# An attention and feed-forward kernel on Trainium2: another order of loads, output additions and remainders at the turns of batches and half batches

## The chip, the cores and the metric

The kernel runs on one core of one Trainium2 chip, as one program of 14,752 profiled instructions. The metric is the device time of one execution in microseconds (us); less is better.

## What is computed

For 8 batches, 8 heads, 576 tokens and a head width of 64, 32 memories per head are formed with softmax weights of `phi`; each token attends to these memories, and the result (4608 x 512) goes through a feed-forward layer (512 to 2048 to 512). All arrays are float32.

```python
a = exp(phi - max(phi, axis=2)); a = a / (sum(a, axis=2) + 1e-9)
k_m, v_m = einsum('bhsm,bhsd->bhmd', a, k), einsum('bhsm,bhsd->bhmd', a, v)
attn = softmax(q @ k_m.T / 8)                 # over the 32 memories
x = (attn @ v_m).transpose(0, 2, 1, 3).reshape(4608, 512)
h = x @ w_in
g = h * clip(h + 3, 0, 6) / 6
out = g @ w_out
```

## The kernel before, in words

**Order.** Every engine executes its instructions in the order in which the program issues them, and that order is written by hand: strings of words such as `fo.C.3` or `fetch.N.0.0` are played as calls. In the tables `FOURTH`, `STEADY` and `EVERY` the numbers are slots 0 to 31 of a batch; C is the batch in work, N the next one, M the one after. `FOURTH` belongs to batch 3, `STEADY` to batches 4 to 7, `EVERY` to all of these; words of batches past the last are dropped. SP (SyncE) issues the DMAs in the same order, so a DMA that waits holds back those behind it. PE is TensorE, DVE is VectorE, ACT is ScalarE, POOL is GpSimd.

**What a slot does.** From batch 3 on (287 us into the span) the loop over `s` (line 1039) makes one slot for each of the 16 blocks of 128 hidden columns in each half batch: slots 0 to 15 for the first half (256 tokens), 16 to 31 for the second (320 tokens, of which 64 are put by). Two slots (k = 0 and 1) make a unit. A slot's order is:

- `gemm1` (L716, six products on TensorE) into one of two PSUM banks; `relu` (L722, ScalarE) and `gate` (L735 and, for the 64 tokens, L739, VectorE);
- in an odd slot `sum_first` (L745, VectorE) and `sum_second` (L749 and L750, GpSimd): sums of the gated blocks for a fast 2 x 2 block multiplication with seven products A11, M5, M2, A22, M6, M7, M1;
- in an even slot `finish_unit(..., 1)` of the unit before, ahead of the slot's words; in an odd slot `finish_unit(..., 0)` of its own unit, behind the slot's words. `finish_unit` splits blocks into a rounded high part (L756, ScalarE) and its remainder (L761, VectorE): three blocks for part 0, which need `sum_first` alone, four for part 1, which need `sum_second` too;
- the words of the slot;
- `half_step(s - 3)`: the products (L688) of the unit three slots back, nine matmuls for part 0 in an odd slot, twelve for part 1 in an even slot. Each of the seven products is a `triple`: high x high, high x low, low x high, so the remainder is needed at the third matmul. Part 1 also fetches the streamed weights (L684) of the unit two ahead; M6, M7 and M1 read such streams. At the turns (slots 0 to 3 and 16 to 19) nothing is fetched, since the next half begins with the units that are still there.

**Leaving.** After a half batch's last unit the sums leave PSUM: `leave_first` in slot 1 or 17, `leave_second` (L795 on ScalarE, L798 and L799 on VectorE) and `leave_third` (L803 and L804 on GpSimd, then the store L806 on SP) in slot 2 or 18, so ahead of slot 3's or 19's `sum_second` on GpSimd. The next half's products take the same four PSUM banks.

**Batches 4 and 6.** In their slots 0 to 2 and after slot 2 the products of the tokens put by are made (`rest_stage`). There the words of slots 0, 1 and 2 are played after its units 3, 4 and 5, and `leave_third` after its unit 2.

**The words that the change moves.** `fetch.N.c.h` (L217) loads half h of weight chunk c (512 KB) from DRAM into one of two buffers: chunks 0 and 2 share one, 1 and 3 the other; `fo` (L428, TensorE) folds the next batch's values into a chunk, `vh` (L439, ScalarE) and `vl` (L448, VectorE, one operand in PSUM) split the result; `bh` (L412, ScalarE) and `bl` (L417, GpSimd) split the second half's probabilities; `xa` (L309, and L306 twice for `xa.N.2`, VectorE) and `xe` (L313, ScalarE) are phi less its maxima and its exponential; `pn` (L225) and `kv` (L238) load phi and k and v; `mt` (L277, VectorE) and `mo` (L283, SP) turn and write out phi's maxima, `sp` (L288, SP) reads them back; `cs` (L391, GpSimd) and `ds`, `dr`, `dm` (L403, GpSimd) belong to the attention's softmax.

## Time and profile before

| | |
|---|---|
| runs | 1340.69, 703.06 and 705.54 us; median 705.54 |
| profiled execution | 705.24 us, of which the span of instructions is 703.2 |
| TensorE busy | 680.7 us, 97% of the span |
| VectorE, ScalarE, GpSimd busy | 532.1, 388.1, 333.0 us |
| granted clock of TensorE | 0.998 on average |
| DMA | 162.86 MB, 232 GB/s |

The profile is of one execution. Times count from the first instruction. In the view of stretches a row is: stretch, its length, busy time of the engine with the number of its instructions, granted clock of TensorE (1.00 is full speed), busy share of the DMA engines, GB/s. In the timeline a row is: start, length, engine, line of the kernel, operation, output<-inputs, shapes, number of instructions merged; in brackets the idle time before it and what ended that. A VectorE or GpSimd instruction that is held up after its start shows a greater length and no idle time. "SPq" is SyncE's queue at the issue of a DMA. The view of waits has: who waited for whom, us in total, times, longest. Slot 0 of batch 5 begins at 452.25, of batch 7 at 615.71; slot 4 of batch 5 at 462.67, of batch 7 at 624.42; slot 5 of batch 4 at 389.66.

### The profile page before, as it was taken

To read this page: it belongs to the slowest core of one execution; us is meant where nothing else is said; L and a number is where in the kernel's file an instruction comes from. 1 tells how busy PE (TensorE), PEld (TensorE's weight loads), DVE (VectorE), ACT (ScalarE), POOL (GpSimd) and SP (SyncE) were. 2 spreads that over 40 slices of the span, in tenths; PEclk is the share of its full clock that TensorE was granted. 3 is DMA by queue.
4 is the path that set the end of the run, shared out by engine and by line. 5 is a ranking of instruction groups with operands and counts; after the bars stand their busy time and mean duration, and the time that the engine had idled before them with its cause. 6 is when DMAs were issued, how large, how long until landed. Compare 5 with 4: busy or idle time off the path is not lost.

```text
span 703.2 us, 14752 instructions
## 1 busy us (share of the span) xinstructions
PE 680.7 (97%) x5622; PEld 577.2 (82%) x5622; DVE 532.1 (76%) x962; ACT 388.1 (55%) x786; POOL 333.0 (47%) x333
## 2 busy tenths in 40 slices
PE   8999999999999999999999999899999999999997
PEld 3456777878877787789889998799988999889997
DVE  4899987776466455566998869977898778987765
ACT  4677785554344455554655655555465555655543
POOL 2645330396564574632545435453457334554433
PEclk9999999999999999999999999999999999999999
DMA  9988573655671784899673877749675593736351
GB/s 353 421 328 314 181 270 125 225 178 178 270 260 47 277 291 132 302 375 343 221 260 118 265 273 271 275 166 332 216 262 191 155 323 114 270 118 219 121 180 47
DMA packets 66270, 162.86 MB, mean 232 GB/s; under 512 B 6808, under 2 KB 13976, under 8 KB 63640
## 3 DMA queue, kind: packets, MB, share of 16 engines
q1 hardware_dynamic: 66120, 161.86, 65.2%
q8 instruction: 44, 0.72, 0.4%
q14 instruction: 26, 0.21, 0.1%
q10 hardware_dynamic: 80, 0.07, 0.0%
HBM read 135.68 MB, written 26.22 MB: 230 GB/s over the span
## 4 chain that ended last, share of the span: by engine, by line
PE 47%; DVE 27%; DMA 9%; ACT 7%; issue 4%; POOL 3%; SPq 2%; ACTq 0%; POOLq 0%; DVEq 0%
PE acc L688 17%; PE acc L545 11%; PE ph L491 7%; PE ph L716 7%; DVE rounded L761 7%; DVE gated L735 3%; DVE gated L745 3%; DVE both L448 2%; DMA stream<-kept 2%; DMA w<-w_kept 2%; ACT rounded L756 2%; PE pk L323 2%; DMA kvt<-in_kv 2%; PE pv L428 2%; DMA kept<-stage 1%
## 5 line engine op out<-in xcount | busy, mean ns | idle before, releaser
L688 PE MATMUL acc<-w,rounded 128*128 128x256 f32 x1248 | 177.7, 282 | 4.4 <-DVE rounded L761 3.8
L688 PEld LDWEIGHTS acc<-w,rounded 128*128 128x128 f32 x1248 | 157.7, 188 | 26.7 <-issue 10.8
L749 POOL TENSOR_TENSOR gated<-gated 128x256 f32<-128x256 f32 x80 | 76.8, 961 | 189.0 <-DVE gated L735 158.2
L761 DVE TENSOR_TENSOR rounded<-gated,rounded 128x384 fp32r<-128x384 f32 (+1 forms) x160 | 133.2, 833 | 38.0 <-ACT rounded L756 32.5
L716 PE MATMUL ph<-probs,both 128*128 128x256 f32 (+1 forms) x960 | 150.4, 292 | 0.0
L756 ACT CAST rounded<-gated 128x384 fp32r<-128x384 f32 (+1 forms) x160 | 90.6, 567 | 95.3 <-DVE gated L745 89.2
L716 PEld LDWEIGHTS ph<-probs,both 128*128 128x128 f32 x960 | 131.6, 188 | 0.2
L722 ACT ACTIVATE gf<-ph,three 128x256 f32<-128x256 f32 (+1 forms) x160 | 79.9, 499 | 42.3 <-PE ph L716 40.7
L545 PE MATMUL acc<-w,ghi 128*128 128x512 f32 x384 | 101.0, 398 | 0.1
L688 PE MATMUL acc<-stream,rounded 128*128 128x256 f32 x720 | 97.3, 279 | 1.5 <-DMA stream<-kept 1.3
L688 PEld LDWEIGHTS acc<-stream,rounded 128*128 128x128 f32 x720 | 88.6, 188 | 3.6 <-DMA stream<-kept 2.5
L545 PEld LDWEIGHTS acc<-w,ghi 128*128 128x128 f32 x384 | 68.9, 188 | 23.9 <-issue 5.7
L735 DVE SCALAR_TENSOR_TENSOR gated<-gf,ph 128x256 f32<-128x256 f32 x160 | 65.5, 410 | 27.0 <-ACT gf L722 26.9
L491 PEld LDWEIGHTS ph<-probs,both 128*128 128x128 f32 x528 | 75.0, 188 | 11.2 <-DVE gf L507 5.2
L491 PE MATMUL ph<-probs,both 128*128 128x256 f32 (+1 forms) x528 | 78.5, 297 | 2.7 <-DVE gf L507 2.6
L507 DVE SCALAR_TENSOR_TENSOR gf<-gf,ph 128x576 f32<-128x576 f32 x44 | 33.0, 750 | 40.8 <-ACT gf L501 40.6
L501 ACT ACTIVATE gf<-ph,three 128x576 f32<-128x576 f32 (+2 forms) x52 | 36.5, 703 | 43.0 <-PE ph L491 38.1
L545 PE MATMUL acc<-w,glo 128*128 128x512 f32 x192 | 54.0, 390 | 0.0
L448 DVE TENSOR_TENSOR both<-pv,both 128x512 fp32r<-128x512 f32 x62 | 42.3, 682 | 14.9 <-ACT both L439 14.7
L525 DVE TENSOR_TENSOR glo<-gf,ghi 128x512 fp32r<-128x512 f32 x44 | 39.1, 892 | 12.8 <-PE acc L545 7.0
L439 ACT CAST both<-pv 128x512 fp32r<-128x512 f32 x62 | 36.1, 584 | 20.7 <-DVE both L448 13.6
L194 POOL TENSOR_TENSOR w<-tmp,raw 128x512 uint32<-128x512 uint32 x14 | 21.8, 1580 | 45.2 <-DVE tmp L184 24.5
(106 smaller groups left out, 886.9 us busy)
## 6 DMA issues: line engine op xcount, KB each, us to landing
stream<-kept SPq DMA_DIRECT2D x186, 256.0 KB, 4.4
kvt<-in_kv SPq DMA_DIRECT2D x32, 516.0 KB, 7.0
w<-w_kept SPq DMA_DIRECT2D x32, 512.0 KB, 6.0
raw<-in_w SPq DMA_DIRECT2D x16, 512.0 KB, 8.6
raw<-in_w SPq DMA_DIRECT2D x8, 1024.0 KB, 7.9
out_t<-o SPq DMA_DIRECT2D x16, 512.0 KB, 3.3
w<-w_kept SPq DMA_DIRECT2D x8, 1024.0 KB, 7.8
kept<-stage SPq DMA_DIRECT2D x24, 256.0 KB, 4.4
```

The source lines that it names most:

```text
L448: nc.vector.tensor_tensor(both[:, 1], src, both[:, 0].bitcast(F32), ALU.subtract)
L491: nc.tensor.matmul(dst, w[:, g, fs], x[:, g * n : (g + 1) * n], start=(i == 0), stop=(i == len(seq) - 1),)
L501: nc.scalar.activation(self.gf, self.h, AF.Relu, bias=three)
L525: nc.vector.tensor_tensor(self.glo[:, :n], self.gated(), self.ghi[:, :n].bitcast(F32), ALU.subtract)
L545: nc.tensor.matmul(accs[self.b, self.rest, k].rearrange("p (x c) -> p x c", c=VC), left[:, t * P : (t + 1) * P], w, start=k in self.first ...
L688: nc.tensor.matmul(dst, left[l], right[r], start=begin and n == 0, stop=end and n == 2, skip_group_check=True)
L716: nc.tensor.matmul(h, w[:, g, fs], x[:, g * self.n : (g + 1) * self.n], start=(i == 0), stop=(i == len(seq) - 1))
L722: nc.scalar.activation(self.gf, self.h[k], AF.Relu, bias=three)
L735: nc.vector.scalar_tensor_tensor(dst, by_tile(self.gf), 6.0, by_tile(self.h[k]), ALU.min, ALU.mult)
L749: nc.gpsimd.tensor_tensor(g[:, 2:4], g[:, 0::8], g[:, 1:8:6], ALU.subtract)
L756: nc.scalar.copy(self.parts[0][:, at], self.g[:, 1:8][:, at])
L761: nc.vector.tensor_tensor(low[:, at], self.g[:, 1:8][:, at], high[:, at].bitcast(F32), ALU.subtract)
```

## The change

Eight edits, all of order; the number and the sizes of the instructions stay.

- The loads of the next batch's first two weight chunks go from slots 5, 7, 9 and 11 to slots 0, 1, 1 and 2 (batches 4 to 7), in batch 3 to 7, 9, 11 and 16. The last half of the fourth chunk goes from slot 29 to 27.
- `vl.C.3.0` goes from slot 0 to 1, `vh.C.3.1` from 3 to 4, `vl.C.3.1` from 4 to 5, `bh.C.1` from 4 to 6, `bl.C.1` from 5 to 7.
- `xa.N.0` goes from 6 to 5, `xe.N.0` from 7 to 6, `xa.N.1` and `xa.N.2` from 8 to 7, `xe.N.1` from 9 to 8.
- `pn.M` goes from 20 to 17, `mt.M` and `mo.M` from 27 to 29, `kv.M.2` from 27 to 28.
- Part 1's products are in the order M6, M7, A22, M1 instead of A22, M6, M7, M1.
- In `leave_second` the addition that reads M6 and M7 comes first, the one that reads M1 second; two quarters of the tile `x` change places for it.
- `leave_third` becomes three steps: `leave_fourth` (the first GpSimd addition) behind `sum_second` of slot 3 or 19, `leave_fifth` (the second) behind that of slot 5 or 21, `store` at the end of slot 6 or 22.
- In batches 4 and 6 and at the end of the program these three steps stay together, after unit 2 of `rest_stage`.

```diff
--- before.py
+++ after.py
@@ -94,18 +94,19 @@
 
 FOURTH = """
 0 to2.7.0 th.7.1 rp.6 fo.C.2 vh.C.2.0 vl.C.2.0 / 1 to2.7.1 vh.C.2.1 vl.C.2.1 / 3 rp.7 / 4 fo.C.3 vh.C.3.0 vl.C.3.0 / 5 vh.C.3.1 vl.C.3.1
+/ 7 fetch.N.0.0 / 9 fetch.N.0.1 / 11 fetch.N.1.0 / 16 fetch.N.1.1
 """
 
 STEADY = """
-0 fo.C.3 vh.C.3.0 vl.C.3.0 / 3 vh.C.3.1 / 4 vl.C.3.1 bh.C.1 / 5 bl.C.1
+0 fetch.N.0.0 fo.C.3 vh.C.3.0 / 1 fetch.N.0.1 vl.C.3.0 fetch.N.1.0 / 2 fetch.N.1.1 / 4 vh.C.3.1 / 5 vl.C.3.1 / 6 bh.C.1 / 7 bl.C.1
 """
 
 EVERY = """
-0 sp.N / 5 fetch.N.0.0 / 6 xa.N.0 / 7 xe.N.0 fetch.N.0.1 / 8 xa.N.1 xa.N.2 / 9 xe.N.1 fetch.N.1.0 / 10 xe.N.2 / 11 mem.N fetch.N.1.1
-/ 12 nr.N nk.N q.N.0 / 13 q.N.1 / 14 tp.N tk.N / 16 sc.N.0 ct.N.0 pt.M / 17 kv.M.0
-/ 20 sc.N.1 ct.N.1 pn.M / 21 cm.N.0 cs.N.0 cm.N.1 kv.M.1 / 22 fo.N.0 vh.N.0.0 vl.N.0.0 / 23 fetch.N.2.0 vh.N.0.1 vl.N.0.1 ex.N.0 cs.N.1 fetch.N.2.1
+0 sp.N / 5 xa.N.0 / 6 xe.N.0 / 7 xa.N.1 xa.N.2 / 8 xe.N.1 / 10 xe.N.2 / 11 mem.N
+/ 12 nr.N nk.N q.N.0 / 13 q.N.1 / 14 tp.N tk.N / 16 sc.N.0 ct.N.0 pt.M / 17 pn.M kv.M.0
+/ 20 sc.N.1 ct.N.1 / 21 cm.N.0 cs.N.0 cm.N.1 kv.M.1 / 22 fo.N.0 vh.N.0.0 vl.N.0.0 / 23 fetch.N.2.0 vh.N.0.1 vl.N.0.1 ex.N.0 cs.N.1 fetch.N.2.1
 / 24 ds.N.0 dr.N.0 dm.N.0 mx.M.0 / 25 fo.N.1 vh.N.1.0 vl.N.1.0 ex.N.1 / 26 vh.N.1.1 vl.N.1.1 mx.M.1 fetch.N.3.0
-/ 27 ds.N.1 dr.N.1 bt.N.0 dm.N.1 mt.M mo.M kv.M.2 / 28 fo.N.2 vh.N.2.0 vl.N.2.0 bh.N.0 / 29 vh.N.2.1 vl.N.2.1 bl.N.0 fetch.N.3.1
+/ 27 ds.N.1 dr.N.1 bt.N.0 dm.N.1 fetch.N.3.1 / 28 fo.N.2 vh.N.2.0 vl.N.2.0 bh.N.0 kv.M.2 / 29 vh.N.2.1 vl.N.2.1 bl.N.0 mt.M mo.M
 / 30 bt.N.1 kv.M.3 / 31 kv.M.4
 """
 
@@ -774,7 +775,7 @@
 
             todo = (
                 (("A11", 0, 1, kept(2)), ("M5", 0, 0, kept(3)), ("M2", 1, 1, kept(0))),
-                (("A22", 2, 1, kept(1)), ("M6", 3, 1, part and stream(1)), ("M7", 3, 0, part and stream(2)),
+                (("M6", 3, 1, part and stream(1)), ("M7", 3, 0, part and stream(2)), ("A22", 2, 1, kept(1)),
                  ("M1", 2, 0, part and stream(0))),
             )[part]
             begun = set()
@@ -787,21 +788,27 @@
             m = sums[self.b, self.half]
             self.x = sb.tile([P, 4, VC], F32, name="o", **O_RING)
             nc.scalar.mul(self.x[:, 0::2], m[0].rearrange("p (x c) -> p x c", c=VC), 1.0 / 6.0)
-            nc.scalar.mul(self.x[:, 3], m[1][:, VC:], 1.0 / 6.0)
+            nc.scalar.mul(self.x[:, 1], m[1][:, VC:], 1.0 / 6.0)
 
         def leave_second(self):
             m, x = sums[self.b, self.half], self.x
             o = self.o = sb.tile([P, 4, VC], F32, name="o", **O_RING)
-            nc.scalar.mul(x[:, 1], m[2][:, VC:], 1.0 / 6.0)
+            nc.scalar.mul(x[:, 3], m[2][:, VC:], 1.0 / 6.0)
             m1 = m[2][:, :VC].unsqueeze(1).broadcast_to([P, 2, VC])
             m67 = m[3].rearrange("p (x c) -> p x c", c=VC)
-            nc.vector.scalar_tensor_tensor(o[:, 0::3], m1, 1.0 / 6.0, x[:, 0::3], ALU.mult, ALU.subtract)
-            nc.vector.scalar_tensor_tensor(o[:, 0::3], m67, 1.0 / 6.0, o[:, 0::3], ALU.mult, ALU.add)
-
-        def leave_third(self):
+            nc.vector.scalar_tensor_tensor(o[:, 0::3], m67, 1.0 / 6.0, x[:, 0:2], ALU.mult, ALU.subtract)
+            nc.vector.scalar_tensor_tensor(o[:, 0::3], m1, 1.0 / 6.0, o[:, 0::3], ALU.mult, ALU.add)
+
+        def leave_fourth(self):
             o, x = self.o, self.x
             nc.gpsimd.tensor_tensor(o[:, 1:3], x[:, 0:2], x[:, 2:4], ALU.add)
-            nc.gpsimd.tensor_tensor(o[:, 0::3], o[:, 0::3], x[:, 1:3], ALU.add)
+
+        def leave_fifth(self):
+            o, x = self.o, self.x
+            nc.gpsimd.tensor_tensor(o[:, 0::3], o[:, 0::3], x[:, 3:1:-1], ALU.add)
+
+        def store(self):
+            o = self.o
             row = self.b * S + OFF[self.half]
             nc.sync.dma_start(
                 out=out[row : row + 2 * P].rearrange("(i p) d -> p i d", i=2),
@@ -1002,6 +1009,8 @@
                 order = list(range(NFT // 2))[:: -1 if half else 1]
                 units += [Unit(b, half, u, len(units) + k) for k, u in enumerate(order)]
 
+        leaving = []
+
         def half_step(i, between=None):
             if i < 0:
                 if i > -4 and i < -1:
@@ -1018,7 +1027,7 @@
             if unit.last:
                 (unit.leave_second if part else unit.leave_first)()
                 if part and not between:
-                    unit.leave_third()
+                    leaving.extend((unit.leave_fourth, unit.leave_fifth, unit.store))
             return unit
 
         def finish_unit(unit, part):
@@ -1053,6 +1062,8 @@
                 if k:
                     unit.sum_first()
                     unit.sum_second()
+                    if len(leaving) > 1:
+                        leaving.pop(0)()
                 elif s >= 2 and not (resting and i == 2):
                     finish_unit(units[s // 2 - 1], 1)
                 if not resting:
@@ -1065,8 +1076,10 @@
             if resting:
                 us[i].prepare()
             unit = half_step(s - LAG - 1, (lambda: (us[3].total(), us[3].prepare())) if resting and i == 2 else None)
+            if not s % 2 and len(leaving) == 1:
+                leaving.pop()()
             if resting and i == 2:
-                after = {2: [unit.leave_third]}
+                after = {2: [unit.leave_fourth, unit.leave_fifth, unit.store]}
                 if b < B:
                     first = units[s // 2 - 1]
                     for k in range(3):
```

## Rows read from the trace of the kernel before

**Rows 1.** Busy time of TensorE by stretches.

```profile
641.46:645.20 3.74, 3.74 (x36) 1.00 0.69 214
416.26:420.39 4.13, 4.13 (x35) 1.00 0.51 194
615.71:618.98 3.27, 3.27 (x37) 1.00 0.43 148
452.25:457.23 4.98, 3.35 (x37) 1.00 0.98 356
462.67:476.44 13.77, 12.80 (x102) 1.00 0.69 239
624.42:637.72 13.30, 12.60 (x102) 1.00 0.56 187
389.66:399.21 9.55, 9.47 (x84) 1.00 0.90 268
522.87:525.36 2.49, 2.19 (x17) 1.00 0.32 27
...
659.42:662.13 2.71, 2.33 (x18) 1.00 0.65 210
```

**Rows 2.** Timeline of SP before the turn to batch 5.

```profile
439.79 1.27 SPq L684 DMA_DIRECT2D stream<-kept  x3
446.03 0.58 SPq L283 DMA_DIRECT2D nmx<-nmxT  x1
...
448.56 0.42 SPq L217 DMA_DIRECT2D w<-w_kept  x1
```

**Rows 3.** Timeline of batch 5, slots 0 to 5.

```profile
454.72 1.09 PE L428 MATMUL pv<-w,kvT 64*32 64x512 f32 x16 [1.64 <-DMA w<-w_kept]
...
463.88 1.29 POOL L804 TENSOR_TENSOR o<-o 128x512 f32<-128x512 f32 x1 [0.25 <-DVE o L799]
464.16 1.29 DVE L745 TENSOR_TENSOR gated<-gated 128x256 f32<-128x256 f32 x1
...
466.92 1.06 PE L688 MATMUL acc<-w,rounded 128*128 128x256 f32 x7 [0.37 <-DVE rounded L761]
```

**Rows 4.** Timeline of batch 4, slots 5 to 9.

```profile
391.56 0.42 DVE L745 TENSOR_TENSOR gated<-gated 128x256 f32<-128x256 f32 x1
...
392.55 0.46 POOL L750 TENSOR_TENSOR gated<-gated 128x128 f32<-128x128 f32 x1
392.57 0.85 DVE L761 TENSOR_TENSOR rounded<-gated,rounded 128x384 fp32r<-128x384 f32 x1 [0.58 <-ACT rounded L756]
...
392.97 1.89 POOL L417 TENSOR_TENSOR probs<-pT,probs 128x640 fp32r<-128x640 f32 x1
...
395.33 0.68 DVE L309 TENSOR_TENSOR pnat<-pnat,nmxb 128x512 f32<-128x512 f32 x1
...
399.71 0.28 DVE L306 TENSOR_TENSOR pnat<-pnat,nmxb 64x128 f32<-64x128 f32 x1
```

**Rows 5.** Timeline of batch 6, slot 2.

```profile
535.68 1.87 PE L688 MATMUL acc<-stream,rounded 128*128 128x256 f32 x9 [0.58 <-DMA stream<-kept]
```

**Rows 6.** Timeline of batch 4, stage of the tokens put by.

```profile
377.89 0.83 DVE L829 TENSOR_TENSOR rounded<-rest,rounded 128x256 fp32r<-128x256 f32 x1
...
378.40 1.47 POOL L804 TENSOR_TENSOR o<-o 128x512 f32<-128x512 f32 x1
378.64 1.37 DVE L829 TENSOR_TENSOR rounded<-total,rounded 128x128 fp32r<-128x128 f32 x1
```

**Rows 7.** Timeline of batch 5, slots 21 and 22.

```profile
507.02 1.04 POOL L391 TENSOR_TENSOR st<-st,mx 128x512 f32<-128x512 f32 x1
...
507.28 1.20 DVE L761 TENSOR_TENSOR rounded<-gated,rounded 128x384 fp32r<-128x384 f32 x1
```

**Rows 8.** Busy time of VectorE, one stretch of batch 5.

```profile
503.40:528.00 24.60, 24.28 (x55) 1.00 0.84 286
```

**Rows 9.** Waits of SP's queue, 287 us to the end.

```profile
SPq L806 <- POOL o L804: 112.0, 10, 12.7
```

## The prediction

> **What bounds the kernel now.** I read first the busy time by stretches, for TensorE alone [rows 1]: its first two rows are a quiet pair of slots of a first and of a second half batch (641.46 and 416.26 us). TensorE is busy in all of their 3.74 and 4.13 us, at full clock, so it is the bound and only its pauses can be won. A pair holds 33 products, 0.113 us each; an even slot of a first half takes 2.04, an odd one 1.70. The other rows are the places where more was taken:
> - slot 0 of batch 5: 4.98 where batch 7 takes 3.27, lost 1.71;
> - slots 4 to 9 of batch 5: 13.77 for 3 x 3.74 = 11.22, lost 2.55; of batch 7: 13.30, lost 2.08;
> - slots 5 to 9 of batch 4: 9.55 for 9.18, lost 0.37 (batch 6 has the same pattern);
> - slot 29 of batch 5: 2.49 for 1.89, lost 0.6 (batches 3 and 4 alike);
> - slot 21 of batch 7: 2.71 for 1.89, lost 0.82.
>
> Then the timelines, for what ended these waits. In slot 0 it is a DMA, the last half of the fourth weight chunk, issued only at 448.56: SP had stood, from 441.06, at the write of the maxima, which went out at 446.03 [rows 2]. The fold starts at 454.72, 6.2 after that issue [rows 3]. In slots 4 to 9 it is VectorE's "rounded" (466.92 in [rows 3]). Behind it lies one pattern. The sum of line 745 takes 1.29 at 464.16 and ends 0.28 after GpSimd's L804 [rows 3]; in a quiet slot it takes 0.42 [rows 4]. VectorE's additions of two SBUF tiles and GpSimd's don't run together. A stream that came late cost batch 6 a wait of 0.58 and stretched a row of nine products to 1.87, where nine fill 1.02 [rows 5]: about 1.3 in all.
>
> **The rule of the port, which carries most terms.** [rows 6]: one VectorE addition, asked for at 377.89, waits until GpSimd's first output addition is over and ends at 378.72; L804, due since 378.40, lasts 1.47; the next VectorE addition, asked for at 378.64, lasts 1.37 and ends at 380.01, just behind L804. So who asks first is served first, and a GpSimd instruction that is due gets in between two VectorE ones. [...]
>
> **Names.** "p0" is the remainder (L761) of the three blocks that an odd slot's products need two slots later, "p1" that of the four blocks needed one slot after. TensorE needs p0 0.91 after that slot begins (eight products). A quiet odd slot is slot 5 of batch 4 [rows 4]: L745 ends at 391.98, GpSimd's L749 holds the port until L750 begins at 392.55, L750 to 393.01, and p0 ends at 393.42. That slot began at 389.66 [rows 1], so p0 is needed at 389.66 + 3.74 + 0.91 = 394.31. Slack 0.9.
>
> **The change, part by part.**
> *GpSimd's two output additions behind the slot's own sums (slots 3 and 5, 19 and 21).* Their number and length stay, 1.29 for the second [rows 3], 1.3 taken for either once it holds the port. Won: L745 in the turning slot runs at once, 0.87 earlier. Lost: the additions now stand in front of p1 of slot 3 and p0 of slot 5.
> *Products M6 and M7 first, and the output's two VectorE additions swapped.* Same work. The bank of M6 and M7 is free one VectorE instruction (0.7) earlier. Whatever of slot 4's share in the 2.55 is owed to that bank goes; it is taken to go whole in the terms below.
> *Remainders and phi.* The fold's first remainder (L448) moves from slot 0 to 1, where it lies in the time that p0 waits for L750 anyway: 0. Its second moves from slot 4 to 5. phi's less_max (L309, 0.68) moves from slot 6 to 5, and its two other parts from 8 to 7 (0.68, and twice 0.28, [rows 4]), all in odd slots ahead of p0. GpSimd's remainder of the probabilities (L417, 1.89, of which 1.44 holding the port) goes from slot 5 to 7.
>
> *Batches 4 and 6, slot 7* (the leaving is done in the remainder stage there). By the order of asking, from L745's end (what each holds the port, [rows 4]): L749 0.56, L309 0.56, L750 0.45, first L306 0.25, L417 1.45, second L306 0.2, p0 0.41: 3.9, where a quiet slot takes 1.44. L745 ends at about 395.9 (slot 5's two extra instructions make it no earlier), p0 at 399.8, needed at 389.66 + 2 x 3.74 + 0.91 = 398.05. A wait of 1.75 and 0.1 to start again, for the 0.37 of before: +1.5 each, **+3.0**. Bounds: 0 (L417 behind p0) to +2.5 each.
>
> *Batch 5, slots 3 to 9* (leaving and phi together). Slot 4 began at 462.67, so slot 5 begins at 464.70 if nothing hinders it. L745 of slot 3 asks at 464.16 [rows 3]; it now runs to 464.55, L749 and L750 to 465.57, p0 465.98; needed at 464.70 + 0.91 = 465.61: lost 0.5. First output addition to 467.25, p1 467.8, needed 467.81. Gate and L745 of slot 5 to 468.65; L749, L750 to 469.65; L309 to 470.25; second output addition to 471.5; p0 471.95, needed 469.85: lost 2.2. Then p1 to 473.05, gate and L745 to 473.9, the pile of slot 7 adds 3.9: 477.8, needed 475.8: lost 2.1. Sum 4.8 for 2.55: **+2.25**. Bounds -0.6 (VectorE served first) to +3.
> *Batch 7, slots 3 to 9* (no phi follows). The same way: 0.5, 0.35, 0.35, 0.4, 0.25, sum 1.9 for 2.08: **-0.2**; bounds -0.8 to +0.5.
>
> *Half turns, slots 19 to 23, of batches 3 to 6.* They lose nothing today. L745 comes about 0.8 earlier, as in slot 3, but p1 then waits for the first addition and ends where it does now. In slot 21 the second addition takes the place that L391 has at 507.02 [rows 7], p0 ends as now, and L391 follows p0 and holds back p1 of slot 22, by 0.5. VectorE is busy or held at the port in 24.28 of the 24.60 us from slot 21 to slot 31 [rows 8], and in slot 29 TensorE waits for it already (0.6, [rows 1]): the lateness comes out there. **+0.4 each, +1.6**; bounds 0 to +0.9 each. Batch 7's slot 21 has nothing behind it: its p0 is 0.8 earlier, **-0.75**; bounds 0 to -0.8.
>
> *Weights at the turn of the batch, and the maxima later.* The last half of the fourth chunk goes ahead of the write of the maxima, so its issue moves from 448.56 to where SP's wait began, 441.06 [rows 2]; with 6.2 to the fold's start it is there at 447.3, well before slot 0 at 452.25. Batch 5 gets 3.27 there, as batch 7: **-1.7**; bounds -1.75 to 0. The first k-v tile goes too, out of the queue before the turn; batch 6's late streams then land in time [rows 5]: **-1.3**; bounds -1.4 to +0.5 (the maxima's write now stands before those streams). The four halves of the next chunks fall in slots 0 to 2, when no stream is fetched, instead of 5 to 11; the third waits for the fold of slot 0, and only the fourth stands behind it, since the next streams are due at slot 4. Streams in slots 4 to 12 land faster, but no wait on them is shown there: 0. In batch 3 they go to slots 7 to 16, needed at 22: 0; bounds -0.5 to +0.5.
> *The transpose of the maxima from slot 27 to 29* (about 0.2 of VectorE): in 27 p0 waits for GpSimd's port anyway, in 29 for L750: 0; bounds -0.6 to +0.2 in three places, from slot 29's row.
> *The store* (L806) held SP's queue 112 us in all for GpSimd's additions [rows 9], streams behind it; it goes behind the streams of slots 4 and 6. Those wait for TensorE at the same time: 0; bounds -0.3 to +0.2. *The second phi load, three slots earlier*: its tile is free since slot 11: 0.
>
> **The sum.** +3.0 +2.25 -0.2 +1.6 -0.75 -1.7 -1.3 = +2.9. The profiled execution took 705.24 us (span 703.2); 705.24 + 2.9 = **708.1**. The median of the runs shown is 705.54, 0.3 off, so nothing is added.
>
> **Rivals.**
> *A. VectorE is served first (faster).* If p0 gets the port before a GpSimd addition that is already due, or L417 falls behind p0, the piles shrink: batch 5 about 2.0 for 2.55, batches 4 and 6 nothing for 0.37, half turns 0, batch 7 -0.8. With the DMAs: -0.55 -0.75 -0.8 -0.75 -1.7 -1.3 = -5.85: **699.4**. For it: GpSimd's starts are rough in a profile. Against it: [rows 6], and L761 of 1.20 behind L391 [rows 7].
> *B. Nothing comes of it.* Half of the piles and half of the gains: **705.2**. For it: VectorE's work is the same to the instruction. Against it: slot 7 has no slack for L417.
> *C. The queue turns against it (slower).* SP stands at the maxima's write until slot 29 and then has a k-v tile, three streams and two megabytes of weights to bring; M6, which is first now, needs its stream 0.34 earlier. Decided by whether the streams issued after that write land before slot 2's products. If not, neither DMA gain comes: 705.24 + 2.9 + 3.0 = **711.1**. Against it: the queue is emptied earlier by a weight half and a k-v tile.
>
> **Chances.** Forecast 0.42, A 0.25, B 0.2, C 0.1, others 0.03. The range is from 699.0 to 712.0: the lower half of A and what exceeds C are left out, less than 0.2. No case comes near 2% of the time (14 us), which is about what a measurement of this kernel tells from no change: faster 0.02, same 0.96, slower 0.02.
>
> **What would show it.** Right: slot 0 of batch 5 near 3.3; L745 near 0.42 in slots 3 and 19; in slot 9 of batches 4, 5 and 6 a wait of TensorE of over a microsecond for "rounded", with p0 of slot 7 ending behind L417; slot 29 of batches 3 to 5 longer than 2.5. Wrong: slot 9 at 1.7 to 2.1 in batches 4 and 6 (then A), or a wait for a stream in slot 2 (then C).

## The result, and the profile after

The changed kernel takes 710.28 us (median of 7 runs, 708.58 to 713.35), the kernel before 705.54. The ratio is 1.0077 with a 95% interval of [1.0049, 1.0104]: a little slower, and inside the 2% that this measurement calls the same. The profiled execution took 713.35 us with a span of 709.8, where the one before had 705.24 and 703.2. Its mean granted clock is 0.992, the lowest of the seven (0.992 to 0.998; 0.998 in the profile before).

The forecast was 708.1 with a range of 699.0 to 712.0. The median lies inside the range, the profiled execution, the longest of the seven, above it. Direction and mechanism were right; two things were missing from the sum. I read the stretches of TensorE first, at the places of [rows 1] and at those that the change touches (columns: start and end, length, TensorE busy with its instructions, granted clock, DMA share, GB/s).

```profile
456.82:460.12 3.30, 3.30 (x37) 1.00 0.87 314
465.56:481.25 15.69, 12.56 (x101) 0.97 0.73 256
633.25:647.84 14.59, 14.23 (x119) 1.00 0.62 199
392.00:397.35 5.35, 5.35 (x50) 1.00 0.69 230
397.35:401.53 4.18, 1.98 (x18) 1.00 0.60 191
401.53:405.17 3.64, 3.64 (x20) 0.53 0.18 46
528.96:531.80 2.84, 2.18 (x17) 1.00 0.99 370
540.37:554.52 14.15, 14.15 (x132) 1.00 0.38 110
667.73:669.62 1.89, 1.89 (x17) 1.00 0.91 266
```

From the top: slot 0 of batch 5 is 3.30 (4.98 before). Slots 4 to 9 of batch 5 are 15.69, and batch 7's slots 4 to 10 are down to 14.59 (15.34 before). The next three rows are the heart of it: in batch 4 TensorE is busy throughout from 392.00, in slot 6, to the end of slot 8; slot 9 takes 4.18 of which TensorE works 1.98, and slot 10, in which it is busy throughout, takes 3.64 for the 2.04 of a quiet one, at a granted clock of 0.53. Slot 29 of batch 5 rose to 2.84, the stage of the tokens put by in batch 6 fell to 14.15, and slot 21 of batch 7 to 1.89. Before, that stage was:

```profile
533.92:549.91 15.99, 15.41 (x132) 1.00 0.23 76
```

Slot by slot, the two profiles differ like this (us; the clock's share is worked out with the third experiment):

| place | predicted | measured | of it the clock |
|---|---|---|---|
| batches 4 and 6, slots 9 and 10 | +3.0 | +3.71 and +3.69 | 2 x 1.55 |
| batch 5, slots 4 to 10 | +2.25 | +3.07 | 1.53 |
| batch 7, slots 4 to 11 | -0.2 | -0.56 | |
| half turns, batches 3 to 6 | +1.6 | +1.95 | |
| batch 7, slot 21 | -0.75 | -0.81 | |
| batch 5, slot 0 | -1.7 | -1.68 | |
| batch 6, stage of the tokens put by | -1.3 | -1.84 | |
| sum | +2.9 | +7.53 | 4.63 |
| the rest of the span | 0 | -0.89 | |

The rest is a wait for a stream in slot 4 of batch 3 (-0.68, a place that differs by as much among the profiles), slot 9 of batch 3 (+0.38; phi's parts moved there too, and without them in slot 7, in experiments 1 and 10, it is 1.70 again), slots 22 to 30 of batch 7 (-0.49, see experiment 9), the last stage (-0.42, which differs by as much among the profiles of one order), and small differences. Together that is the 6.6 us by which the spans differ. Without the clock the terms sum to +2.90.

The timeline of batch 4 from slot 6 on shows how slot 9 came about (columns: start, length, engine, line and operation, operands; in brackets the idle time before it and who ended it). All lines of the changed kernel behind the words are one higher than before: L746 is the L745 of [rows 4], L762 the L761. GpSimd's two output additions, L803 and L804 before, are L804 and L808.

```profile
394.28 0.72 ACT L413 CAST probs<-pT 128x640 fp32r<-128x640 f32 x1
...
394.91 0.62 ACT L314 ACTIVATE pnat<-pnat 128x512 f32<-128x512 f32 x1
...
395.44 0.46 ACT L723 ACTIVATE gf<-ph,three 128x256 f32<-128x256 f32 x1
...
395.93 0.42 DVE L736 SCALAR_TENSOR_TENSOR gated<-gf,ph 128x256 f32<-128x256 f32 x1 [0.82 <-ACT gf L723]
...
396.38 0.42 DVE L746 TENSOR_TENSOR gated<-gated 128x256 f32<-128x256 f32 x1
...
396.72 1.23 DVE L310 TENSOR_TENSOR pnat<-pnat,nmxb 128x512 f32<-128x512 f32 x1
...
397.37 0.91 POOL L751 TENSOR_TENSOR gated<-gated 128x128 f32<-128x128 f32 x1
...
397.88 2.10 DVE L307 TENSOR_TENSOR pnat<-pnat,nmxb 64x128 f32<-64x128 f32 x2
...
398.24 1.59 POOL L418 TENSOR_TENSOR probs<-pT,probs 128x640 fp32r<-128x640 f32 x1
...
400.00 0.56 DVE L762 TENSOR_TENSOR rounded<-gated,rounded 128x384 fp32r<-128x384 f32 x1
...
400.62 1.07 PE L689 MATMUL acc<-w,rounded 128*128 128x256 f32 x7 [2.20 <-DVE rounded L762]
401.53 1.29 PE L717 MATMUL ph<-probs,both 128*128 128x256 f32 x6
```

The pile is the predicted one. From the end of L746 (396.80) to the end of p0 (400.56) it takes 3.76 where 3.9 was forecast. L310 stretches to 1.23 beside GpSimd, the two L307 to 2.10, because L418 comes in between, and p0 gets the port last. What was not predicted stands in the first four lines. ScalarE does L413 and L314 one behind the other in slot 6, the relu L723 waits for them, VectorE's gate L736 waits 0.82 for the relu, and L746 ends at 396.80, 0.55 ahead of slot 9, where the forecast had 395.9, 1.24 ahead of it.

The half turn of batch 5, in the same view, VectorE and GpSimd alone, answers to [rows 7]:

```profile
506.78 0.42 DVE L746 TENSOR_TENSOR gated<-gated 128x256 f32<-128x256 f32 x1
...
508.17 1.61 POOL L804 TENSOR_TENSOR o<-o 128x512 f32<-128x512 f32 x1
...
509.01 1.32 DVE L762 TENSOR_TENSOR rounded<-gated,rounded 128x512 fp32r<-128x512 f32 x1
...
512.84 1.29 POOL L808 TENSOR_TENSOR o<-o 128x512 f32<-128x512 f32 x1
...
513.11 1.44 DVE L762 TENSOR_TENSOR rounded<-gated,rounded 128x384 fp32r<-128x384 f32 x1
...
514.09 1.37 POOL L392 TENSOR_TENSOR st<-st,mx 128x512 f32<-128x512 f32 x1
```

L746 of slot 19 runs at once, in 0.42. Then each of the three GpSimd instructions stretches one remainder: L804 p1 of slot 19, L808 p0 of slot 21, and L392, pushed behind p0, p1 of slot 22 (1.07 at 514.93). That is the chain that the forecast wrote down, and slot 29 pays for it.

SP's queue before batch 5 answers to [rows 2]:

```profile
444.79 0.42 SPq L218 DMA_DIRECT2D w<-w_kept  x1
...
454.84 0.58 SPq L284 DMA_DIRECT2D nmx<-nmxT  x1
```

The last half of the fourth chunk is issued at 444.79, 12.03 ahead of slot 0 where it was 3.69 ahead, and 10.05 before the write of the maxima behind which it used to stand.

### The profile page after: what moved, and what is told of

It is laid out like the page before. It is cut to its first block, busy times and chain, and to the rows that moved or that the text cites. A ratio compares the mean times of both kernels' runs of the same rounds, so it can differ in the third digit from the quotient of the medians.

```text
span 709.8 us, 14802 instructions
## 1 busy us (share of the span) xinstructions
PE 683.3 (96%) x5618; PEld 580.8 (82%) x5622; DVE 537.9 (76%) x962; ACT 386.9 (55%) x786; POOL 339.0 (48%) x333
## 4 chain that ended last, share of the span: by engine, by line
PE 62%; DVE 17%; DMA 8%; ACT 5%; POOL 3%; issue 3%; SPq 1%; ACTq 0%; POOLq 0%; DVEq 0%
PE acc L689 25%; PE ph L717 13%; PE acc L546 11%; PE ph L492 7%; DVE rounded L762 4%; PE pv L429 3%; DMA stream<-kept 2%; DMA qh<-in_qt 2%; PE pk L324 2%; DVE pnat L307 1%; DVE gated L736 1%; DMA kept<-stage 1%; DVE both L449 1%; DMA w<-w_kept 1%; DVE gf L508 1%
## 5 line engine op out<-in xcount | busy, mean ns | idle before, releaser
L762 DVE TENSOR_TENSOR rounded<-gated,rounded 128x384 fp32r<-128x384 f32 (+1 forms) x160 | 138.1, 864 | 31.7 <-ACT rounded L757 25.5
L717 PE MATMUL ph<-probs,both 128*128 128x256 f32 (+1 forms) x960 | 152.2, 294 | 0.0
L717 PEld LDWEIGHTS ph<-probs,both 128*128 128x128 f32 x960 | 133.3, 190 | 0.2
L689 PE MATMUL acc<-stream,rounded 128*128 128x256 f32 x720 | 113.1, 284 | 1.1 <-DMA stream<-kept 1.1
L689 PEld LDWEIGHTS acc<-stream,rounded 128*128 128x128 f32 x720 | 96.9, 191 | 14.7 <-issue 8.7
L723 ACT ACTIVATE gf<-ph,three 128x256 f32<-128x256 f32 (+1 forms) x160 | 80.0, 500 | 44.9 <-PE ph L717 43.5
L736 DVE SCALAR_TENSOR_TENSOR gated<-gf,ph 128x256 f32<-128x256 f32 x160 | 65.6, 410 | 35.4 <-ACT gf L723 35.2
L195 POOL TENSOR_TENSOR w<-tmp,raw 128x512 uint32<-128x512 uint32 x14 | 21.8, 1577 | 44.8 <-DVE tmp L185 19.4
```

The source lines that it names most:

```text
L689: nc.tensor.matmul(dst, left[l], right[r], start=begin and n == 0, stop=end and n == 2, skip_group_check=True)
L717: nc.tensor.matmul(h, w[:, g, fs], x[:, g * self.n : (g + 1) * self.n], start=(i == 0), stop=(i == len(seq) - 1))
L723: nc.scalar.activation(self.gf, self.h[k], AF.Relu, bias=three)
L736: nc.vector.scalar_tensor_tensor(dst, by_tile(self.gf), 6.0, by_tile(self.h[k]), ALU.min, ALU.mult)
L762: nc.vector.tensor_tensor(low[:, at], self.g[:, 1:8][:, at], high[:, at].bitcast(F32), ALU.subtract)
```

## The experiments

Four questions were open: is the pile in slot 7 made by the order of asking at the port; what do ScalarE and the clock add; which of the DMA moves brings the two gains; and what are the other moves worth. Each edit is made on the changed kernel, unless said otherwise. Of the tables' long lines the diffs show only the words that differ.

**1. phi's parts one slot later** (out of slot 7, L418 stays).

```diff
-/ 7 xa.N.1 xa.N.2 / 8 xe.N.1
+/ 8 xa.N.1 xa.N.2 / 9 xe.N.1
```

> Phi's two less_max parts back in slot 8, behind p1, and their exponential back in slot 9; GpSimd's L418 stays in slot 7. Theory (the port serves in the order of asking, and three VectorE additions and GpSimd's L418 alternate ahead of p0): p0 of slot 7 is asked for before L418, ends about 1.45 after L746, and slot 9 of batches 4, 5 and 6 takes 1.7 to 2.1 instead of 4.2 to 4.9. Slot 10 returns to 2.04 (from 2.9 to 3.6), since TensorE no longer pauses. About 3.5 less in each of three batches: 10 less than the changed kernel's profile, ratio to the kernel before 0.992 to 0.996. Rival (L418 in slot 7 is harmful by itself): slot 9 stays above 3. Rival (the clock falls for a reason of its own): slot 10 stays above 2.8 although slot 9 is short.

Measured: 702.4 us, ratio 0.9948 [0.9933, 0.9963]. Stretches of slots 9 and 10 of batch 4, then slot 9 of batch 5 (batch 6 has 1.87):

```profile
398.00:399.85 1.85, 1.85 (x17) 1.00 0.75 260
399.85:402.47 2.62, 2.52 (x20) 1.00 0.44 131
473.68:475.78 2.10, 2.00 (x18) 1.00 1.00 304
```

Timeline of its batch 4:

```profile
397.04 0.42 DVE L746 TENSOR_TENSOR gated<-gated 128x256 f32<-128x256 f32 x1
...
398.05 0.85 DVE L762 TENSOR_TENSOR rounded<-gated,rounded 128x384 fp32r<-128x384 f32 x1 [0.58 <-ACT rounded L757]
...
398.44 1.88 POOL L418 TENSOR_TENSOR probs<-pT,probs 128x640 fp32r<-128x640 f32 x1
...
399.18 1.70 DVE L762 TENSOR_TENSOR rounded<-gated,rounded 128x512 fp32r<-128x512 f32 x1
```

The pause in slot 9 is gone, and so is the lower clock. From L746's end to p0's end it takes 398.90 - 397.46 = 1.44, the figure of a quiet slot, with the same L418 in the same slot: p0 asks before L418 is due and goes first. L418 then stretches p1 to 1.70 and slot 10 to 2.62, which I had not foreseen; it is what the order of asking gives, one instruction further on.

**2. L418 two slots later** (phi's parts stay in slot 7).

```diff
-/ 6 bh.C.1 / 7 bl.C.1
+/ 6 bh.C.1 / 9 bl.C.1
```

> GpSimd's L418 from slot 7 to slot 9; phi's less_max stays in slot 7 ahead of p0. VectorE's order is that of the changed kernel to the instruction. Theory: of the pile of slot 7 only L418's 1.45 goes; p0 is asked for behind three additions that alternate with L750 and L751, ends about 2.4 after L746 instead of 3.9, and slot 9 of batches 4 and 6 takes about 1.9; batch 5, which comes late to it, 2 to 2.8. Slot 10 returns to 2.04. Ratio to the kernel before 0.993 to 0.998. Rival (VectorE's own work ahead of p0 is what is too much): slot 9 stays above 3.5.

Measured: 703.15 us, ratio 0.9962 [0.9947, 0.9976]. Stretches of slots 9 and 10 of batch 4, and its timeline:

```profile
397.11:400.05 2.94, 1.99 (x17) 1.00 0.77 247
400.05:402.09 2.04, 2.04 (x20) 1.00 0.10 37
```

```profile
397.64 0.85 DVE L307 TENSOR_TENSOR pnat<-pnat,nmxb 64x128 f32<-64x128 f32 x2
...
398.52 0.56 DVE L762 TENSOR_TENSOR rounded<-gated,rounded 128x384 fp32r<-128x384 f32 x1
```

The two L307 fall from 2.10 to 0.85, and the pile from 3.76 to 2.5 (L746 ends at 396.57, p0 at 399.08); 2.4 was expected. The slot is 1.0 longer than expected, 0.7 of it since L746 is as late as in the changed kernel (0.54 ahead of slot 9): this is what ScalarE keeps. Moving either part away, phi or L418, shortens slot 9, to 1.85 and 2.94; it is the two together that make 3.76.

**3. Products in the pause.** In slot 9 of batches 4 to 6 the slot's six products of L717 are made three times. The output is not changed by it; there are 36 more products of 0.113 us.

```diff
                 unit.gemm1(k)
+                if i == 9 and b in (4, 5, 6):
+                    unit.gemm1(k)
+                    unit.gemm1(k)
                 unit.relu(k)
```

> The changed kernel, but in slot 9 of batches 4, 5 and 6 TensorE makes its six first products three times over (the same values into the same bank): 36 products more, 4.1 us of work that nobody needs, 1.36 in each of three slots that hold a pause of about 2.2. Theory (the granted clock falls to its lower level after that pause, and slot 10 is longer for that): slot 9 keeps its length of 4.2 to 4.9, the pause is 0.8, slot 10 returns to 2.04 at full clock, and the kernel gets 3 to 4.5 faster than the changed one for having more to do. Rival (slot 10 is long because VectorE is late there): slot 10 stays at 2.9 to 3.6 and the time stays or rises by up to 4.

Measured: 707.43 us (10 runs), ratio 1.0023 [1.0013, 1.0033], which lies below the changed kernel's interval. Stretches of slots 9 and 10 of batch 4:

```profile
398.51:402.74 4.23, 3.35 (x29) 1.00 0.65 188
402.74:404.78 2.04, 2.04 (x20) 1.00 0.00 0
```

Slot 9 stays as long (4.23 for 4.18: the products fill the pause), but TensorE works 3.35 in it and not 1.98, and slot 10 runs at full clock. Slots 9 and 10 together take 6.27, 6.49 and 6.27 in batches 4, 5 and 6, where the changed kernel's profile has 7.82, 8.02 and 7.82. The lower clock thus costs 1.55, 1.53 and 1.55, in sum 4.63 of the profile's 6.6. The medians differ by 2.85 us only, which fits that not every execution has all three falls.

**4. The half turns leave at once.** In the first halves of batches 3 to 6 both GpSimd additions and the store go back into slot 18.

```diff
                 if part and not between:
-                    leaving.extend((unit.leave_fourth, unit.leave_fifth, unit.store))
+                    steps = (unit.leave_fourth, unit.leave_fifth, unit.store)
+                    if unit.half == 0 and unit.b < B - 1:
+                        for step in steps:
+                            step()
+                    else:
+                        leaving.extend(steps)
```

> The changed kernel, but at the half turns of batches 3 to 6 the two output additions and the store stand in slot 18 as before; batch 7 and the turns of batches keep the new place. Theory (the second addition in slot 21 pushes L392 in front of p1 of slot 22, and VectorE, which has no gap until slot 31, carries the lateness to slots 27 and 29): slot 27 returns from 2.03 to 1.89 and slot 29 from 2.85 to 2.49 (2.17 to 1.89 in batch 6), 0.5 in each of four batches, 2.0 in all, about 0.3%. Rival (slots 27 and 29 are longer for the later transpose of the maxima): they stay at 2.03 and 2.85.

Measured: 709.22 us, ratio 1.0043 [1.0028, 1.0058]. In its profile slot 27 is back at 1.89 and slot 29 of batch 4 is 2.55:

```profile
448.87:451.42 2.55, 2.17 (x18) 1.00 0.97 360
```

Three falls of the clock remain. The intervals of this kernel and the changed one overlap, so the size is taken from the slots: 27 and 29 together fall by 0.42 to 0.44 in each of the four batches, 1.73 in all, where the change had added 1.95 and the forecast 1.6.

**5. The maxima back in slot 27**, behind the fourth chunk's last half; so their write is again ahead of the k-v tile.

```diff
-/ 27 ds.N.1 dr.N.1 bt.N.0 dm.N.1 fetch.N.3.1 /
+/ 27 ds.N.1 dr.N.1 bt.N.0 dm.N.1 fetch.N.3.1 mt.M mo.M /
...
-/ 29 vh.N.2.1 vl.N.2.1 bl.N.0 mt.M mo.M
+/ 29 vh.N.2.1 vl.N.2.1 bl.N.0
```

> The changed kernel, but the transpose of the maxima and their write are back in slot 27, behind the load of the last half of the fourth chunk and ahead of the k-v tile. Theory (what shortens slot 0 of batch 5 is that this load goes ahead of SP's wait for the write, and what shortens the stage of batch 6 that the queue is emptier by it and by the k-v tile): slot 0 of batch 5 stays at 3.3; the stage of batch 6 (14.15 in the changed kernel, 15.99 before) takes 14.1 to 15.2, since the k-v tile stands behind the wait again. Slots 27 and 29 stay as they are (2.03 and 2.85). Rival (the later write is what helps, whatever the order): slot 0 goes back to above 4.5. Rival on slot 29 (the transpose costs there): it changes by more than 0.15.

Measured: 711.75 us, ratio 1.0082 [1.0055, 1.0108], the same as the changed kernel within the intervals. Slot 0 of batch 5 is 3.30 and batch 6's stage 14.15 here too: for both gains the weight half ahead of the write is enough, without the k-v tile. (The phi load in slot 17 is in this kernel too and was not taken back by itself.) Slots 27 and 29 keep their lengths, so the transpose of the maxima costs nothing in slot 29. In this profile slot 9 of batches 4 and 6 is 4.19, as long as the changed kernel's in batch 4, and slot 10 behind it 2.04 at full clock; only batch 5, with a slot 9 of 5.13, has a fall. Slots 9 and 10 of batch 4:

```profile
397.77:401.96 4.19, 1.99 (x17) 1.00 0.58 190
401.96:404.00 2.04, 2.04 (x20) 1.00 0.00 0
```

**6. The first weights at the turn, alone**, built on the kernel before: chunks 0 and 1 in slots 0 to 2 (in batch 3 in 7 to 16), nothing else.

```diff
-0 fo.C.3 vh.C.3.0 vl.C.3.0 / 3 vh.C.3.1
+0 fetch.N.0.0 fo.C.3 vh.C.3.0 vl.C.3.0 / 1 fetch.N.0.1 fetch.N.1.0 / 2 fetch.N.1.1 / 3 vh.C.3.1
...
-0 sp.N / 5 fetch.N.0.0 / 6 xa.N.0 / 7 xe.N.0 fetch.N.0.1 / 8 xa.N.1 xa.N.2 / 9 xe.N.1 fetch.N.1.0 / 10 xe.N.2 / 11 mem.N fetch.N.1.1
+0 sp.N / 6 xa.N.0 / 7 xe.N.0 / 8 xa.N.1 xa.N.2 / 9 xe.N.1 / 10 xe.N.2 / 11 mem.N
```

> The kernel before with one part of the change alone: the first two weight chunks of the next batch are loaded in slots 0 to 2 (batch 3: 7 to 16) instead of 5 to 11. Theory (no wait on these loads or on the streams of slots 4 to 12 is shown, so nothing is won): every slot from 4 to 12 keeps its length within 0.1, ratio to the kernel before 0.999 to 1.002; slot 0 of batch 5 stays at 4.98 and the stage of batch 6 at 16.0 or gets up to 0.5 longer, since those loads come behind the same full queue. Rival (the loads compete with the streams in slots 4 to 12): those slots lose 0.3 to 1 in all, ratio 0.998 or less.

Measured: 705.89 us (10 runs), ratio 1.000 [0.9983, 1.0017]. Stretches of batch 4's stage and of slot 0 of batch 5, then two lines of batch 5's timeline, SP and TensorE:

```profile
371.17:386.33 15.16, 15.15 (x132) 1.00 0.47 140
452.68:459.26 6.58, 4.40 (x37) 0.83 0.99 371
```

```profile
452.85 0.43 SPq L218 DMA_DIRECT2D w<-w_kept  x1
...
455.70 1.09 PE L429 MATMUL pv<-w,kvT 64*32 64x512 f32 x16 [2.18 <-DMA w<-w_kept]
```

The new load at 452.85 runs beside the late half of the fourth chunk. The fold then waits 2.18, where it waited 1.64 [rows 3], and the clock falls behind that (0.83 over the slot), which makes most of the slot's 1.6 more; 4.98 had been expected to stay. The stage of batch 4 is 1.0 longer. Slots 4 to 12, out of which the loads were taken, are no shorter. So in this profile, the longest execution of the ten, these loads win nothing and cost at two places; the median shows no loss. In the changed kernel, where the fourth chunk comes early, slot 0 is 3.30 with the same loads.

**7. phi's exponential out of slot 6.** L314 goes to slot 7, behind the two VectorE parts.

```diff
-/ 6 xe.N.0 / 7 xa.N.1 xa.N.2
+/ 7 xa.N.1 xa.N.2 xe.N.0
```

> The changed kernel, but ScalarE's first exponential of phi (L314, 0.62) stands in slot 7 behind relu instead of in slot 6 ahead of it. Theory (L413 and L314 in slot 6 hold back relu of slot 7, so that L746 ends 0.9 later than counted, at 396.80 for 395.9): L746 of slot 7 is asked for 0.4 to 0.7 earlier, all of the pile with it, and slot 9 of batches 4 and 6 shrinks by as much, from 4.2 and 4.9 to between 3.5 and 4.4; the clock may still fall. Rival (VectorE alone sets when the pile begins): L746 and slot 9 stay within 0.15.

Measured: 706.42 us (8 runs), ratio 1.0022 [1.0001, 1.0042]. Slot 9 of batch 4, and the gate and the sum of slot 7:

```profile
397.02:400.69 3.67, 1.98 (x17) 1.00 0.71 217
```

```profile
395.07 0.42 DVE L736 SCALAR_TENSOR_TENSOR gated<-gf,ph 128x256 f32<-128x256 f32 x1 [0.30 <-ACT gf L723]
...
395.53 0.42 DVE L746 TENSOR_TENSOR gated<-gated 128x256 f32<-128x256 f32 x1
```

VectorE waits 0.30 for the relu and not 0.82. L746 is 1.49 ahead of slot 9's start, for 397.35 - 396.38 = 0.97 in the changed kernel, and slot 9 is 3.67 for 4.18: 0.5 of the lateness is L314's; the rest, by the timeline, is L413's, which was not moved by itself. Slot 10 of batches 4 and 6 is 2.04 with the shorter pause; in batch 5 (slot 9 4.96) it is 2.82.

**8. Old product order and old order of VectorE's two output additions.**

```diff
-("M6", 3, 1, part and stream(1)), ("M7", 3, 0, part and stream(2)), ("A22", 2, 1, kept(1)),
+("A22", 2, 1, kept(1)), ("M6", 3, 1, part and stream(1)), ("M7", 3, 0, part and stream(2)),
...
-nc.vector.scalar_tensor_tensor(o[:, 0::3], m67, 1.0 / 6.0, x[:, 0:2], ALU.mult, ALU.subtract)
-nc.vector.scalar_tensor_tensor(o[:, 0::3], m1, 1.0 / 6.0, o[:, 0::3], ALU.mult, ALU.add)
+nc.vector.scalar_tensor_tensor(o[:, 0::3], m1, 1.0 / 6.0, x[:, 0::3], ALU.mult, ALU.subtract)
+nc.vector.scalar_tensor_tensor(o[:, 0::3], m67, 1.0 / 6.0, o[:, 0::3], ALU.mult, ALU.add)
```

> The changed kernel with part 1's products in the old order (A22 first) and the output's two VectorE additions in the old order; the leaving stays spread. Theory (this part alone takes the wait for the bank of M6 and M7 out of slot 4): slot 4 of batch 5 goes from 2.05 back to about 2.33, of batch 7 from 2.05 to about 2.46; slot 21 of batch 7 stays at 1.89; 0.7 in all, too little for the time. Rival (slot 4 is short because L746 and GpSimd no longer collide): slot 4 stays at 2.05.

Measured: 708.69 us in one run. Slots 4 and 5 of batch 5 (in batch 7 they are 2.35 and 1.97):

```profile
464.24:466.55 2.31, 2.31 (x20) 1.00 0.99 397
466.55:468.57 2.02, 2.00 (x17) 1.00 0.81 235
```

In the changed kernel slot 4 is 2.05 in both batches and slot 5 is 2.35. What M6 and M7 in front win in slot 4, slot 5 gives back, since there p0 is late anyway: by this profile worth nothing.

**9. All leaving at once, new product order.** Both GpSimd additions and the store back in slots 2 and 18 of every half batch.

```diff
-                    leaving.extend((unit.leave_fourth, unit.leave_fifth, unit.store))
+                    for step in (unit.leave_fourth, unit.leave_fifth, unit.store):
+                        step()
```

> The changed kernel with both output additions and the store back in slots 2 and 18; the order of the products stays new. Theory: L746 of the turning slot lasts about 1.27 again behind the second addition; slot 21 of batch 7 goes from 1.89 back to about 2.7 and slot 5 of batches 5 and 7 from 2.35 to between 2.6 and 2.85, while slot 4 stays at 2.05; slot 29 of batches 3 to 5 goes from 2.85 to about 2.5. In batch 5 slot 7 has no second addition ahead of it. Rival (the old order of products caused the length of slot 21): slot 21 stays at 1.89.

Measured: 712.71 us in one run, beside 713.35 for the changed kernel's profile, with the same three falls of the clock. Slot 21 of batch 7 and slot 5 of batch 5:

```profile
666.71:669.47 2.76, 2.38 (x18) 1.00 0.65 201
467.15:470.34 3.19, 2.26 (x17) 1.00 0.78 272
```

Slot 21 of batch 7 loses its 0.81 again, which shows whose gain that was. In batches 5 and 7 slot 5 rises to 3.19 and 3.18, more than I expected, and slots 7 to 11 behind it fall. Slots 22 to 30 behind it are 0.49 longer as well: slot 22 takes 2.29 for 2.23 and slot 23 1.94 for 1.89, with TensorE busy throughout. So it is in the three profiles in which slot 21 has its pause (the kernel before, experiments 6 and 9) and in none of the nine others; why, no run shows. Against the changed kernel's profile, spreading the additions gains 0.86 in slot 21 of batch 7 and 0.49 behind it, about 0.4 at batch 5's turn and nothing at batch 7's (slot 5 gains 0.83, slots 7 to 11 lose 0.85), and costs 1.8 in the half turns: in sum about nothing. That the profile of this experiment is 0.7 longer in its span comes from the stream in slot 4 of batch 3 (+0.42) and the last stage (+0.39).

**10. What holds, in one version.** phi's parts as in experiment 1, L413 in slot 8 and L418 in slot 9, the half turns as in experiment 4, all else as in the changed kernel.

```diff
-/ 6 bh.C.1 / 7 bl.C.1
+/ 8 bh.C.1 / 9 bl.C.1
...
-/ 7 xa.N.1 xa.N.2 / 8 xe.N.1
+/ 8 xa.N.1 xa.N.2 / 9 xe.N.1
```

> The changed kernel with three of its parts taken back or moved on: phi's two less_max parts in slot 8 and its exponential in slot 9, L413 and L418 in slots 8 and 9 (so L418 stands behind the sums of slot 9, whose p0 has the memories' matmuls as slack), the half turns of batches 3 to 6 leaving in slot 18. Kept: the loads at the turn, the order of the maxima, M6 first, the leaving spread at the turns of batches and of batch 7's halves. Theory: slot 9 of batches 4 to 6 at 1.7 to 1.9, slot 10 at 2.04, slots 27 and 29 as before; against the first kernel -1.7 (slot 0), -1.8 (stage of batch 6), -0.8 (slot 21 of batch 7), -2 (slots 4 to 9), together 6 to 7 less: ratio 0.989 to 0.993, faster than either kernel. Rival (the pile comes back elsewhere): a slot between 5 and 12 takes over 0.5 more.

Measured: 697.66 us (697.02 to 697.96), ratio 0.9884 [0.9867, 0.9901], the fastest of all. Its slot 0 of batch 5, slots 9 and 10 of batch 4, and slots 4 to 9 of batch 5:

```profile
452.55:455.82 3.27, 3.27 (x37) 1.00 1.00 329
397.73:401.47 3.74, 3.74 (x35) 1.00 0.66 213
461.26:474.01 12.75, 11.99 (x101) 1.00 0.84 286
```

Slots 9 and 10 have the 3.74 of a quiet pair, and slots 4 to 9 of batch 5 are 1.02 below [rows 1]. Against the profile before, slot 0 brings 1.71, batch 6's stage 1.84, slot 21 of batch 7 0.81, batch 5 1.02, slots 9 of batches 4 and 6 0.37 each, batch 7's slots 4 to 13 0.70 and its slots 22 to 30 0.49: 7.31 of the 7.6 by which the slots differ. The last stage is 0.43 shorter too, but it is 21.4 in some profiles of the changed order and 21.8 in others (experiments 2, 7 and 8), so this is no gain of the order. What is left to win is mainly slots 5 and 7 of batch 5 (2.36 and 2.37 for 1.70), slot 5 of batch 7 (2.33) and slot 29 of batches 3 to 5 (2.53 to 2.55 for 1.89).

## Why the prediction was right, and where it was not

**The port's order of asking: right.** The pile in slot 7 was forecast at 3.9 and is 3.76. Experiments 1 and 2 take one or the other part away and shrink it to 1.44 and 2.5, as the same order says. Rival A, VectorE served first, gave slot 9 as 1.7 to 2.1 in batches 4 and 6; it is 4.18 and 4.93, so A falls.

**Its start: wrong, a term missing.** The step that failed is "L745 ends at about 395.9 (slot 5's two extra instructions make it no earlier)". I asked which VectorE and GpSimd instructions stand ahead of L745 and not what ScalarE has to do before the relu. The change had put L412 (now L413, 0.72), from slot 4, and L313 (now L314, 0.62), from slot 7, into the same slot 6, ahead of that relu. L746 ends at 396.80; 0.21 of the 0.9 between is that this whole profile is later by then (slot 5 begins at 389.87 for 389.66), so against its slots the sum is 0.7 late. Without the clock batches 4 and 6 lost 7.40 - 3.10 = 4.3 for the 3.0 forecast; experiment 7 gets 0.5 of it back in each by moving L314. The rest, L413's share, rests on the timeline.

**The clock: not in the sum.** Behind the pause in slot 9 the granted clock fell to the lower level of 1.2 GHz, 0.53 on the mean of slot 10, and slots 9 and 10 lost about 1.5 more, three times in the profile. This is the largest error of the forecast. With it taken out the terms sum to +2.90, the forecast's +2.9, but that agreement is luck: +1.3 in batches 4 and 6, +0.35 in the half turns, -0.7 in batch 5, -0.5 in batch 6's stage and -0.4 in batch 7 cancel. Experiment 3 shows the clock's part: p0 is as late as before, TensorE is kept busy while it waits, the clock stays at 1.00, and the kernel with 36 products more is the faster one. The Trainium skill tells of the effect behind longer waits: "TensorE: Matmul & The Clock Gate", section "HAM oscillation — how this bites in real kernels", has matmuls start at half clock after a wait for data. The case agrees in kind, with the 0.53 behind a pause of 2.20, but not each time: experiment 5 has the same 4.19 in slot 9 and 2.04 behind it.

**Batch 5, slots 3 to 9: right in sign, mis-sized.** The forecast had slot 5 lose 2.2, with the second output addition and L309 (now L310) ahead of p0, each in turn. In the run L310 went ahead of GpSimd's L751, and p0 ahead of the second addition (L808), so slot 7 lost only 0.68 (2.38 for the quiet 1.70). Slot 9 lost more instead, 2.73 without the clock (4.43 in experiment 3) for 2.1: L746 ends only 0.34 ahead of it, at 476.08. That is not ScalarE's alone here, since p1, which L808 stretched to 1.43, ends at 475.10 and the relu at 475.16, and experiment 7 shortens this pause only from 2.39 to 2.23. Without the clock the place cost 1.54 for 2.25.

**M6 and M7 first: worth nothing.** The share of slot 4 that I took to go whole did go (2.31 to 2.05) and came back in slot 5 (experiment 8), since the wait there was for p0 and not for the bank.

**Half turns: right.** L746 is at 0.42, and then L804, L808 and L392 (before: L391) stretch p1, p0 and p1, in the slots named. It comes out in slots 27 and 29, at 0.43 to 0.52 a batch for 0.4.

**The DMA terms: right, with one reason too many.** Slot 0 of batch 5 gains 1.68 (1.7 forecast), batch 6's stage 1.84 (1.3). Both are there when the weight half goes ahead of the write of the maxima. The forecast also credited batch 6's gain to the k-v tile ahead of that write; experiment 5 shows that the gain does not need it. The weights at the turn were put at nothing; experiment 6 finds no gain in slots 4 to 12, and a loss of 1.6 in slot 0 of batch 5 where the fourth chunk is late, in one profile. Rival C needed a wait for a stream in slot 2; the stage is busy throughout (14.15 of 14.15), so C falls. Rival B had half of everything, which no place shows.

**Slot 21 of batch 7: right**, 0.81 for 0.75, and it goes with the leaving (experiment 9), as do 0.49 in the slots behind it, which the forecast did not have.

What stays open: which pauses bring the clock down. Batch 5's, the longest of a profile (2.23 to 2.41), did so in all six that have it (the changed kernel, experiments 4, 5, 7, 8 and 9); those of batches 4 and 6 (2.19 to 2.21) did in the changed kernel and experiments 4 and 9, and not in experiments 5 and 8.

## What to carry to other kernels

When an instruction moves to another slot, write out every engine's queue ahead of the chain that TensorE waits for: here two ScalarE instructions that met in one slot delayed a VectorE sum that the move never touched. At a port that VectorE and GpSimd share, ask for each GpSimd addition which VectorE addition will be next to ask: the cheap place is where that one has slack. Count a pause of TensorE with what may follow it at the lower clock, and move a load ahead of a DMA that waits before looking for a better slot for it.

## What the runs showed that was not expected

A pause of 2.20 us in slot 9 brought slot 10, in which TensorE never waits, from 2.04 to 3.64 us at a granted clock of 0.53. Making 12 needless products in each of three such pauses took the median from 710.28 to 707.43 us. And the fall is not certain: in the profile of experiment 5 one of three such pauses brought it, in that of the changed kernel all three, and the seven executions of the changed kernel have mean granted clocks from 0.992 to 0.998.
